# Linear attention and a Mish feed-forward in one kernel: the first loads in one queue and in other buffers, VectorE's work of a tile in other slots

## The chip, the cores and the metric

The kernel runs on one core of one Trainium2 chip. The metric is the device time of one execution in microseconds (us). TensorE (PE) multiplies, VectorE (DVE) and ScalarE (ACT) do the elementwise work, SyncE (SP) issues nearly all DMAs, GpSimd (POOL) only clears a few constants at the start. Each engine runs its instructions in the order in which the program lists them.

## The reference, cut to what matters

```python
kv  = einsum('bhsd,bhse->bhde', k, v)               # 8 batches, 8 heads, 576 tokens, head size 64
out = einsum('bhsd,bhde->bhse', q, kv)
rms = sqrt(mean(out * out, axis=-1) + 1e-6)
x   = (out / rms * g_norm) as [4608 tokens, 512]
h   = x @ w_in                                      # w_in 512 x 2048, float64 in memory
g   = h * tanh(log1p(exp(h)))                       # Mish
return g @ w_out                                    # w_out 2048 x 512, float64 in memory
```

## The kernel before, in words

Both large products are done by a scheme of Strassen's kind: seven block products instead of eight, on sums and differences of blocks. Each factor is split into a high part (`hi`, rounded to the matmul's format by a cast on ACT) and a rest (`lo`, a subtraction on DVE), and a product is three matmuls. So each operand costs one ACT cast and one DVE subtraction in `split` (lines 117 and 118).

**Part 1** makes h and Mish for 9 tiles of 512 tokens. A tile has 4 groups of 7 products: 28 **slots** a round, 9 rounds. A slot runs first the evictions that fall due (`evict`), then its product on PE (12 matmuls, line 472), then what the plan holds for that slot (`plan`, filled by `at(slot, f)`, in order of registration). This order, written out by hand, is the order on every engine; no planner moves anything. The evictions of a group are three copies and a Mish on ACT (lines 435, 440, 449, 114) and three additions on DVE (line 492, "put 11", "put 12", "put 22"). The product of A22 of a group is made two slots into the next group and accumulates onto the bank that "put 22" reads, so it waits for that addition.

In round j the kernel also prepares the x of tile j+1 ("attention", line 601), in two units of 4 heads: `load` of q (line 280, 4 or 8 DMAs), `transpose` on DVE (line 285), `halves` (a split), `project` on PE with the kept k-v products, `square` on ACT, `scaled` on DVE (line 324), `squares` (a split), `sums` on PE, `rstd` on ACT, `keep` (the factors to DRAM, line 361), `spread` (back to all partitions, line 368), `normalize` on DVE (line 376). Then `x_form` makes the seven operands of the tile (lines 390 to 409). Beside that, per round, the k-v products of one batch (`k_load`, `k_product`, `kv_keep`, line 232 on PE), and "out" chunks that turn a part of w_out into its seven block forms and store them in DRAM (line 198).

**Float64 weights** come as pairs of 32-bit words. `weight_forms` has the steps LOAD (4 DMAs of 256 KB, line 134), SCALE on ACT (line 139), JOIN (three DVE instructions on the raw words, lines 144 to 146), DIFF (154 to 156), BLOCKS and SUMS (splits). w_in has 8 chunks, of which group n of a tile uses 2n and 2n+1. Their raw words lie in one buffer of the pool `w64` (chunk 1 in a free `gf` buffer); the next LOAD can begin when the JOIN before it has read that buffer.

**Before slot 0** the kernel makes the x of tile 0 in one go (lines 530 to 575). The w_in and q loads go out on SP, those of the first k and v on ACT (`kv_load(nc.scalar, ...)`).

**Part 2** (from `part2`) makes the second product, g @ w_out, from what part 1 stored.

Of the kernel before, what the change touches and what calls it, by code (L numbers as in the profile page):

```python
# [26 lines left out]
def linear_attention_rms_mish_ffn(  # L27
# [239 lines left out]
    def unit_steps(j, u):  # L267
        st = {}

        def load():  # L270
# [77 lines left out]
        def rstd():  # L348
# [183 lines left out]
    kv0 = [kv_load(nc.scalar, 0, 4 * n, 4, [t for m in range(2) for t in (rooms[2 * n + m], rrooms[2 * n + m])]) for n in range(2)]
# [1 line left out]
    weights(1, LOAD)
# [66 lines left out]
    def attention(j):
# [6 lines left out]
        late = 2 if j == 1 else 0  # L608
        for u, n, *names in (
            (0, -19, "load"), (0, -1, "transpose"), (0, 0, "halves"), (1, 1, "load"), (0, 3, "project"),  # L610
            (0, 5, "square", "scaled"), (0, 6, "squares"), (1, 7, "transpose"), (0, 8, "sums"), (1, 9, "halves"),
            (1, 11, "project"), (1, 12, "square", "scaled"), (1, 13, "squares"), (1, 15, "sums"), (1, 16, "rstd"),
            (1, 17, "keep"), (0, 19, "spread0"), (0, 24, "normalize"), (1, 25, "normalize"),
        ):
            at(max(t + n + (late if n < 19 else 0), 0), lambda u=u, names=names: do(j, u, *names))
# [253 lines left out]
```

## Time and profile before

| | us |
|---|---|
| median of 3 runs (946.39 to 953.22) | 952.05 |
| the profiled execution, its own time | 948.55 |
| its span | 946.8 |
| PE busy in the span | 846.3 |
| DVE busy | 610.7 |
| ACT busy | 461.2 |
| mean granted TensorE clock, of full speed | 0.955 |

The span is what the profiler sees of the kernel; 1.75 us of the execution's time lie around it. Busy shares are averages over parts with different limits, so the prediction reads the kernel in stretches: the time up to the first product, then rounds, then part 2. PEclk in a row is the clock that TensorE was granted, 1.00 being 2.4 GHz and 0.50 being 1.2 GHz.

### The profile page before, as it was taken

The page shows a single profiled execution, that of the slowest core. Times are in us where ns is not written, and L with a number is a line of the kernel's source. Part 1 is how long each engine was busy: PE and PEld are TensorE (multiplying, and loading weights), DVE is VectorE, ACT ScalarE, POOL GpSimd, SP SyncE. Part 2 cuts the span into 40 slices and gives each one's busy share as a digit, 9 for nine tenths or more (in the row PEclk, how much of TensorE's full clock was granted, in tenths as well). Part 3 has the DMA queues.
Part 4 walks back from the last instruction along what each step waited for, and adds up shares of the span by engine and source line. Part 5 has one row for each costly group of instructions (what it writes and reads, how often), then busy time and mean ns, then how long its engine had stood idle before and what let it go on. Part 6 is the DMA issues. An engine that isn't in the chain of part 4 may idle for free. (4 is left out here: it accounts for less than half of the span.)

```text
span 946.8 us, 17029 instructions
## 1 busy us (share of the span) xinstructions
PE 846.3 (89%) x6940; PEld 809.7 (86%) x6940; DVE 610.7 (64%) x808; ACT 461.2 (49%) x698; POOL 4.3 (0%) x21
## 2 busy tenths in 40 slices
PE   2457598989799898979989979999999999999997
PEld 1246488989799898979989969999999999999997
DVE  2488567495674747567585435877667777667762
ACT  1445356656465665636666524444444344444341
POOL 1000000000000000000000000000000000000000
PEclk9769799999899899998999989999999999999999
DMA  9465666877869578668665799445443345443331
GB/s 251 118 177 153 198 197 194 238 240 233 237 211 282 173 231 275 198 196 226 205 182 173 248 402 388 146 135 166 129 129 113 112 149 163 122 125 111 113 111 45
DMA packets 157133, 177.40 MB, mean 187 GB/s; under 512 B 18752, under 2 KB 138560, under 8 KB 156032
## 3 DMA queue, kind: packets, MB, share of 16 engines
q1 hardware_dynamic: 153856, 173.97, 60.0%
q10 hardware_dynamic: 3200, 2.36, 1.0%
q8 instruction: 54, 0.88, 0.4%
q14 instruction: 23, 0.19, 0.1%
HBM read 114.30 MB, written 62.00 MB: 186 GB/s over the span
## 5 line engine op out<-in xcount | busy, mean ns | idle before, releaser
L697 PE MATMUL a<-wf,gf 128*128 128x256 f32 x1632 | 201.8, 283 | 0.5 <-DVE ur L728 0.5
L697 PEld LDWEIGHTS a<-wf,gf 128*128 128x128 f32 x1632 | 198.4, 192 | 0.7 <-DVE ur L728 0.7
L472 PE MATMUL a<-gf,wf 128*128 128x256 f32 x1296 | 180.3, 295 | 15.6 <-DVE gf L374 10.0
L118 DVE TENSOR_TENSOR gf<-g,gf 128x1024 fp32r<-128x1024 f32 (+1 forms) x123 | 132.9, 1087 | 87.9 <-ACT gf L117 87.9
L472 PEld LDWEIGHTS a<-gf,wf 128*128 128x128 f32 x1296 | 169.9, 201 | 19.5 <-issue 11.5
L472 PE MATMUL bc<-gf,wf 128*128 128x256 f32 x1296 | 174.7, 287 | 11.3 <-ACT ur L440 6.6
L472 PEld LDWEIGHTS bc<-gf,wf 128*128 128x128 f32 x1296 | 164.3, 194 | 16.8 <-ACT ur L440 6.8
L117 ACT CAST gf<-g 128x1024 fp32r<-128x1024 f32 (+1 forms) x123 | 114.4, 939 | 90.2 <-DVE g L677 65.1
L697 PE MATMUL bc<-wf,gf 128*128 128x256 f32 x1224 | 152.7, 283 | 0.1
L697 PEld LDWEIGHTS bc<-wf,gf 128*128 128x128 f32 x1224 | 149.4, 192 | 0.3 <-ACT gf L117 0.3
L472 PE MATMUL a<-a,wf 128*128 128x256 f32 x432 | 68.2, 314 | 38.5 <-DVE ur L492 38.5
L472 PEld LDWEIGHTS a<-a,wf 128*128 128x128 f32 x432 | 63.1, 217 | 44.0 <-DVE ur L492 41.0
L114 ACT ACTIVATE ur<-ur 128x1024 f32<-128x1024 f32 x36 | 38.1, 1058 | 52.7 <-DVE ur L492 52.7
L440 ACT COPY ur<-bc 128x512 f32<-128x512 f32 (+1 forms) x53 | 27.4, 517 | 39.7 <-PE bc L697 23.0
L492 DVE TENSOR_TENSOR ula<-bc,ula 128x512 f32<-128x512 f32 x36 | 24.8, 688 | 31.7 <-PE bc L472 13.8
L117 ACT CAST gf<-a 128x1024 fp32r<-128x1024 f32 x17 | 17.9, 1051 | 53.4 <-DVE a L674 53.4
L117 ACT CAST gf<-gf 128x512 fp32r<-128x512 f32 x45 | 27.0, 619 | 31.5 <-DVE gf L396 15.7
L118 DVE TENSOR_TENSOR gf<-gf 128x512 fp32r<-128x512 f32 x45 | 30.9, 688 | 17.1 <-ACT gf L117 17.1
L449 ACT COPY ur<-a 128x512 f32<-128x512 f32 (+1 forms) x53 | 27.5, 518 | 29.2 <-PE a L697 24.6
L118 DVE TENSOR_TENSOR fl<-fa,fh 128x1024 fp32r<-128x1024 f32 x28 | 34.2, 1221 | 11.3 <-ACT fh L117 11.3
L117 ACT CAST fh<-fa 128x1024 fp32r<-128x1024 f32 x28 | 29.2, 1043 | 10.5 <-DVE fa L285 9.7
L114 ACT ACTIVATE ula<-ula 128x512 f32<-128x512 f32 x36 | 22.7, 630 | 22.0 <-DVE ula L492 21.9
(130 smaller groups left out, 842.2 us busy)
## 6 DMA issues: line engine op xcount, KB each, us to landing
g<-gd SPq DMA_DIRECT2D x18, 2048.0 KB, 8.8
gd<-ur SPq DMA_DIRECT2D x36, 512.0 KB, 4.0
wod<-wst SPq DMA_DIRECT2D x16, 896.0 KB, 4.9
wf<-wod SPq DMA_DIRECT2D x8, 1792.0 KB, 14.4
gd<-ula SPq DMA_DIRECT2D x36, 256.0 KB, 3.9
gd<-ulb SPq DMA_DIRECT2D x36, 256.0 KB, 5.2
w<-in_moe_w_out_dram SPq DMA_DIRECT2D x32, 256.0 KB, 4.4
w<-in_moe_w_in_dram SPq DMA_DIRECT2D x28, 256.0 KB, 3.9
```

The source lines that it names most:

```text
L114: nc.scalar.activation(o, i, AF.Mish)
L117: nc.scalar.copy(hi, src)
L118: nc.vector.tensor_sub(lo, src, hi.bitcast(F32))
L440: then(t + 2, lambda: nc.scalar.copy(dst(st, "22"), st["c"]))
L449: then(t + 4, lambda: nc.scalar.copy(dst(st, "12"), st["a"]))
L472: nc.tensor.matmul(bank[:, jj], w[:, right, a, kc, :], xf[:, b, kc, :], start=first and jj == kc == s == 0, stop=(kc == 1 and s == 2), ski ...
L492: nc.vector.tensor_add(o, bank, o)
L697: nc.tensor.matmul(bank, gf[:, a, c, :], wo[c][:, right, b, :], start=first and c == s == 0, stop=(c == NF2 - 1 and s == 2), skip_group_ch ...
```

## The change

Before slot 0, all loads are issued on SP, in the order w_in chunk 0, k and v of heads 0 to 3, w_in chunk 1, q of unit 0, k and v of heads 4 to 7, q of unit 1, the norm's weights, w_in chunks 2 and 3. Chunks 1 to 3 and the second q go into buffers of the pool `wfp` (name `wf`) that hold no forms yet; the `gf` buffer `w1_room` is gone. DIFF, BLOCKS and SUMS of chunk 0 and SCALE and JOIN of chunk 1 stand ahead of the first transpose; SCALE, JOIN and DIFF of chunk 2 are done before slot 0.

In the rounds, steps stand in other slots: for tile 2 and later `transpose` of unit 0 in slot 20 of the round before (from 27), its `halves` in 25 (from 28), `normalize` in 23 and 24 (from 24 and 25), the operands in 24 to 31 (from 25 to 32), `kv_keep` in 14 (from 24), k-v products in 3, 6, 9, 12 (from 13, 16, 19, 22). The 16 out chunks begin in slots 6, 13, 20 of rounds 1 and 2 and in 9, 15 of rounds 3 to 7 (from every twelfth slot). Three names of buffers (`fh`, `fl`, `fa`) are swapped to fit.

```diff
-        def load():
-            t = qs[u] = att.tile([P, 2, T // R * D], F32, name="qs")
+        def load(t=None):
+            t = qs[u] = att.tile([P, 2, T // R * D], F32, name="qs") if t is None else t
...
-            t = att.tile([P, 2, T], F32, name="fh" if j < T32 else "fa")
+            t = att.tile([P, 2, T], F32, name="fh" if j < T32 else "fl")
...
-    w1_room = fp.tile([P, 4, 2 * P, 2], U32, name="gf")
...
+    early = {j: wfp.tile([P, 4, 2 * P, 2], U32, name="wf") for j in range(1, 4)}
+    early_q = wfp.tile([P, 2, T // R * D], F32, name="wf")
...
+    def k_first(n):
+        kv0.append(kv_load(nc.sync, 0, 4 * n, 4, [t for m in range(2) for t in (rooms[2 * n + m], rrooms[2 * n + m])]))
     weights(0, LOAD)
-    kv0 = [kv_load(nc.scalar, 0, 4 * n, 4, [...]) for n in range(2)]
+    k_first(0)
+    weights(1, LOAD)
     do(0, 0, "load")
-    weights(1, LOAD)
+    k_first(1)
+    units[0][1]["load"](early_q)
...
+    weights(2, LOAD)
+    weights(3, LOAD)
     kv_tiles()
...
     weights(0, SCALE, JOIN)
     kv_product(0, 0, 4, *kv0[0])
     kv_keep(0, slice(0, 2))
-    weights(0, DIFF)
-    do(0, 0, "transpose")
...
-    do(0, 0, "project")
-    weights(0, BLOCKS)
+    weights(0, DIFF, BLOCKS, SUMS)
+    weights(1, SCALE, JOIN)
+    do(0, 0, "transpose", "project")
+    weights(1, DIFF, BLOCKS)
     kv_product(0, 4, 4, *kv0[1])
     kv_keep(0, slice(2, 4))
     do(0, 0, "square", "sums")
-    weights(0, SUMS)
-    do(0, 1, "transpose", "project", "square")
+    weights(1, SUMS)
+    k_load(1, 0)
     k_load(1, 1)
+    weights(4, LOAD)
+    do(1, 0, "load")
+    do(0, 1, "transpose", "project")
     do(0, 0, "rstd")
...
+    weights(2, SCALE)
+    do(0, 1, "square", "sums")
     do(0, 0, "normalize")
+    weights(2, JOIN)
     x_form(A11)
+    do(0, 1, "rstd", "normalize")
     x_form(S1)
+    weights(2, DIFF)
+    for f, n in ((S2, 0), (A12, 1), (S4, 2), (S3, 3), (A22, 5)):
+        at(n, lambda f=f: x_form(f))
+    at(0, lambda: weights(2, BLOCKS, SUMS))
+    for j in range(3, NF2):
+        t = 3 * (j - 3) + 1
+        if 4 <= j < NF2 - 1:
             at(t + 1, lambda j=j: weights(j + 1, LOAD))
         for s, n in ((SCALE, 0), (JOIN, 0), (DIFF, 1), (BLOCKS, 1), (SUMS, 2)):
             at(t + n, lambda j=j, s=s: weights(j, s))
...
+        loads = (5, 6, 14, 16) if b == 2 else (20 - NS, 22 - NS, 5, 8) if b == 3 else (11 - NS, 15 - NS, 5, 8)
-            at(t + (13, 16, 19, 22)[p], lambda b=b, p=p: k_product(b, p))
-        at(t + 24, lambda b=b: kv_keep(b, slice(0, NKC)))
+            at(t + ((12, 14, 16, 18) if b == 2 else (3, 6, 9, 12))[p], lambda b=b, p=p: k_product(b, p))
+        at(t + (20 if b == 2 else 14), lambda b=b: kv_keep(b, slice(0, NKC)))
...
+            (0, 8 - NS if j > 2 else 9 - NS, "load"), (0, 20 - NS, "transpose"), (1, 22 - NS, "load"), (0, 25 - NS, "halves"),
+            (0, 0, "project"), (0, 3, "square", "scaled"), (0, 4, "squares"), (1, 5, "transpose"), (0, 6, "sums"),
+            (1, 8, "halves"), (1, 10, "project"), (1, 12, "square", "scaled"), (1, 13, "squares"), (1, 15, "sums"),
+        )
+        for u, n, *names in steps + ((1, 16, "rstd"), (1, 18, "keep"), (0, 19, "spread0"), (0, 23, "normalize"), (1, 24, "normalize")):
-        for f, n in zip(MADE, (25, 26, 27, 28, 29, 30, 32)):
+        for f, n in zip(MADE, (24, 26, 28, 29, 30, 30, 31)):
             at(t + n, lambda f=f: x_form(f))
...
-    for i in range(2 * NF2):
-        for s, n in zip(range(7), (-13, 0, 0, 1, 2, 3, 6)):
+    places = [NS * j + n for j in range(1, NT - 1) for n in ((6, 13, 20) if j < 3 else (9, 15))]
+    for i, t in enumerate(places):
+        for s, n in zip(range(7), (-12, 0, 0, 1, 2, 3, 5)):
```

## Rows read from the trace of the kernel before

**Rows 1.** Busy time by stretch: us, then PE, PEld, DVE, ACT, POOL, clock, DMA.
```profile
0.00:46.30 46.30, 16.52 (x96) 8.07 (x97) 16.54 (x22) 14.30 (x22) 4.33 (x21) 0.88 0.74 189
46.30:137.70 91.40, 64.46 (x509) 55.87 (x510) 64.56 (x89) 44.67 (x66) 0.00 (x0) 0.82 0.61 175
193.30:248.00 54.70, 51.60 (x451) 48.91 (x450) 35.28 (x54) 32.44 (x51) 0.00 (x0) 0.97 0.82 245
577.80:946.80 369.00, 363.58 (x3026) 363.00 (x3025) 256.73 (x275) 151.13 (x209) 0.00 (x0) 1.00 0.43 135
```
**Rows 2.** Timeline of PE, end of round 1: start, duration, instruction, idle time before.
```profile
199.84 2.93 PE L472 MATMUL a<-a,wf 128*128 128x256 f32 x12 [2.73 <-DVE ur L492]
202.57 1.72 PE L472 MATMUL a<-gf,wf 128*128 128x256 f32 x12
...
205.67 3.04 PE L472 MATMUL bc<-gf,wf 128*128 128x256 f32 x24
208.55 3.04 PE L472 MATMUL a<-gf,wf 128*128 128x256 f32 x24
```
**Rows 3.** Timeline of DVE, the same place.
```profile
197.97 1.24 DVE L285 STREAM_TRANSPOSE fa<-qs 128x1024 f32<-128x1024 f32 x1
199.13 0.65 DVE L492 TENSOR_TENSOR ur<-a,ur 128x512 f32<-128x512 f32 x1
```
**Rows 4.** Busy time, seven stretches of three products, the last and the sum.
```profile
474.52:484.24 9.72, 6.35 (x38) 5.95 (x38) 8.03 (x12) 6.44 (x11) 0.00 (x0) 0.82 0.71 183
sum 76.05, PE 47.24 PEld 44.29 DVE 63.55 ACT 47.32 POOL 0.00; mean PE 6.75 PEld 6.33 DVE 9.08 ACT 6.76 POOL 0.00
```
**Rows 5.** Busy time, the eighth such stretch.
```profile
526.14:531.33 5.19, 4.71 (x38) 4.43 (x38) 3.48 (x6) 4.35 (x8) 0.00 (x0) 1.00 0.28 113
```
**Rows 6.** Timeline of ACT before slot 0.
```profile
11.98 0.60 ACTq L212 DMA_DIRECT2D ulb<-in_v_dram  x1
12.77 1.13 ACT L139 ACTIVATE fl<-w 128x1024 f32<-128x1024 f32 x1 [10.74 <-DMA ula<-in_v_dram]
...
26.26 0.53 ACT L249 COPY kvf<-s 64x128 f32<-64x128 f32 x2 [8.16 <-PE s L232]
...
35.98 1.06 ACT L353 ACTIVATE fa<-fa 128x1024 f32<-128x1024 f32 x1
```
**Rows 7.** Timeline of PE before slot 0 and in round 0.
```profile
20.09 3.75 PE L308 MATMUL x<-fh,kvf 128*128 128x512 f32 x4 [5.50 <-DVE fh L285]
...
46.31 2.90 PE L472 MATMUL a<-gf,wf 128*128 128x256 f32 x12 [9.97 <-DVE gf L374]
...
68.28 1.12 PE L232 MATMUL s<-vm,km 128*64 128x64 f32 x16 [8.62 <-DMA vm<-in_v_dram]
...
113.29 2.93 PE L472 MATMUL a<-a,wf 128*128 128x256 f32 x12 [10.59 <-DVE ur L492]
```
**Rows 8.** What the spread's transfers (line 368) took: min, median, max.
```profile
DMA to landing us min/median/max: 3.8/5.2/6.5
```
**Rows 9.** DMA of the first 24 us.
```profile
DMA packets 5857, 6.01 MB, mean 250 GB/s; under 512 B 1370, under 2 KB 5466, under 8 KB 5857
```
**Rows 10.** Timeline of all engines, one chunk of w_in to the next.
```profile
69.01 1.23 DVE L146 SCALAR_TENSOR_TENSOR fl<-w,fl 128x1024 uint32<-128x1024 uint32 x1
...
70.30 2.44 SPq L134 DMA_DIRECT2D w<-in_moe_w_in_dram  x4
...
76.67 1.16 ACT L139 ACTIVATE fl<-w 128x1024 f32<-128x1024 f32 x1
...
79.85 1.22 DVE L146 SCALAR_TENSOR_TENSOR fl<-w,fl 128x1024 uint32<-128x1024 uint32 x1
```
**Rows 11.** Timeline of DVE before slot 0.
```profile
41.20 1.40 DVE L374 SCALAR_TENSOR_TENSOR gf<-x,gcol,fa 128x512 f32<-128x512 f32 x2
```
**Rows 12.** Busy time of DVE on a chunk of w_in: us, DVE, clock, DMA.
```profile
13.90:20.90 7.00, 6.75 (x9) 1.00 1.08 265
```
**Rows 13.** Busy time in round 8 around PE's longest wait there, seven products.
```profile
547.16:566.55 19.39, 12.60 (x85) 12.19 (x83) 4.78 (x13) 4.97 (x12) 0.00 (x0) 0.82 1.01 406
```

More of the change, by code (lines that the diff above doesn't have):

```diff
@@ L289, in parts @@
             hi = att.tile([P, 2, T], F32R, name="fh")
-            lo = att.tile([P, 2, T], F32R, name="fl")
+            lo = att.tile([P, 2, T], F32R, name="fa")
             split(hi, lo, t)
@@ L315, in square @@
         def square():
-            st["s"] = att.tile([P, 2, T], F32, name="fh" if j == 0 and u else "fa")
+            st["s"] = att.tile([P, 2, T], F32, name="fl" if j >= T32 else "fh" if j == 0 and u else "fa")
             if "x2" in st:
@@ L354, in rstd @@
                 return
-            r = st["r"] = att.tile([H, T], F32, name="fa")
+            r = st["r"] = att.tile([H, T], F32, name="fa" if j < T32 else "fl")
             nc.scalar.preload_act_table_set("natural_log_exp_and_others")
@@ L510, in linear_attention_rms_mish_ffn @@
     rrooms = [up.tile([SL, 4, D], F32, name=n) for n in ("ula", "ula", "ulb", "ulb")]
+    early = {j: wfp.tile([P, 4, 2 * P, 2], U32, name="wf") for j in range(1, 4)}
+    early_q = wfp.tile([P, 2, T // R * D], F32, name="wf")
     def w64_room():
         return pools["w64"].tile([P, 4, 2 * P, 2], U32, name="w64")
-    conv = {j: weight_in(j, (lambda: w1_room) if j == 1 else w64_room) for j in range(NF2)}
+    conv = {j: weight_in(j, (lambda j=j: early[j]) if 0 < j < 4 else w64_room) for j in range(NF2)}
     LOAD, SCALE, JOIN, DIFF, BLOCKS, SUMS, STORE = range(7)
@@ L530, in linear_attention_rms_mish_ffn @@
     nc.scalar.preload_act_table_set("natural_log_exp_and_others")
+    kv0 = []
+    def k_first(n):
+        kv0.append(kv_load(nc.sync, 0, 4 * n, 4, [t for m in range(2) for t in (rooms[2 * n + m], rrooms[2 * n + m])]))
     weights(0, LOAD)
[L532 removed]
+    k_first(0)
+    weights(1, LOAD)
     do(0, 0, "load")
[L534 removed]
+    k_first(1)
+    units[0][1]["load"](early_q)
+    for r in (slice(0, D), slice(D, P)):
+        nc.sync.dma_start(gcol[r, :], g_norm.rearrange("(p o) -> p o", o=1))
+    weights(2, LOAD)
+    weights(3, LOAD)
     kv_tiles()
@@ L607, in attention @@
         t = NS * (j - 1)
[L608 to L615, printed above, removed]
-        for f, n in zip(MADE, (25, 26, 27, 28, 29, 30, 32)):
+        steps = (
+            (0, 1, "transpose"), (1, 3, "load"), (0, 5, "project"), (0, 7, "square", "scaled"), (1, 7, "transpose"),
+            (0, 9, "sums"), (1, 11, "project"), (1, 13, "square", "scaled"), (1, 15, "sums"),
+        ) if j == 1 else (
+            (0, 8 - NS if j > 2 else 9 - NS, "load"), (0, 20 - NS, "transpose"), (1, 22 - NS, "load"), (0, 25 - NS, "halves"),
[3 more added lines that the diff above has]
+        for u, n, *names in steps + ((1, 16, "rstd"), (1, 18, "keep"), (0, 19, "spread0"), (0, 23, "normalize"), (1, 24, "normalize")):
+            at(t + n, lambda u=u, names=names: do(j, u, *names))
+        for f, n in zip(MADE, (24, 26, 28, 29, 30, 30, 31)):
             at(t + n, lambda f=f: x_form(f))
@@ L631, in run @@
                 conv["out", i][s]()
-            at(max(NS - 2, NS + 6 + 12 * i + n), run)
+            at(max(NS - 2, t + n), run)
     wo = [None] * NF2
```

24 lines of the change are left out of this document (2 added, 22 removed).

## The prediction

> **What bounds the kernel now.** I read busy time by stretch first [rows 1]. Part 2, 369 us of the span, has PE busy for 363.6 at clock 1.00: the change touches nothing there, so its time stays. Two stretches are not bound by PE. The first 46.3 us run to the first product; round 0 then takes 91.4 us with PE busy for 64.5 and DVE for 64.6. A later round takes 54.7 us, PE busy for 51.6.
>
> Next the timeline of PE at a round's end [rows 2]. PE waits 2.73 us for DVE's line 492, and the 12 matmuls behind it take 2.93 us; at full pace 24 take 208.55 − 205.67 = 2.88, so a product takes 1.44. The reader should see two losses: the wait, and a product at half clock after it. DVE shows the cause [rows 3]: the addition that PE waits for ("put 22") stands behind the next tile's transpose, and behind that the operands of slots 25 to 32. The seven ends of rounds 0 to 6, measured over the same three products (slots 29 to 31 and their like), take 76.05 us [rows 4] where 7 × 3 × 1.44 = 30.2 would do: 45.8 us are lost. The eighth end takes 5.19, loses 0.9 and keeps clock 1.00 [rows 5]. That one has the same operands to make, but no further tile's transpose and halves, no `kv_keep` and no out chunk. It is the nearest thing the trace has to the changed order.
>
> Last the start [rows 6, 7]: SCALE of chunk 0 begins at 12.77, once ACT has issued its last DMA (11.98 to 12.58); the first product waits for `normalize` until 46.31. In round 0 PE waits 8.62 us for a v load and 10.59 for put 22, the latter held up by a late chunk of w_in.
>
> **The change, part by part.**
>
> *Ends of rounds.* Per tile, transpose and `halves` of unit 0 (1.24 us on DVE each, the halves as the transpose) and `kv_keep` leave slots 24 to 28, the normalisations and operands start one slot earlier, and S1 is made before put 22 falls due. From slot 28 on DVE has put 22 first, then one or two operands a slot. So each of the seven ends should look like the eighth: 7 × 0.9 = 6.1 us remain. The ends of rounds 1 and 2 get a third out chunk in slots 20 to 23. With three evictions, the transpose, two normalisations, a `halves` and two operands, some 14.5 us of DVE work stand in eight slots of 1.44, 11.5 us. Put 22 is then 3 us late and has two products (2.9 us) of slack. I charge 1.5 us to each of the two. Gain 45.8 − 6.1 − 3 = **36.7 us**; ends of the unknown: 45.8 (nothing left) and 23 (half stays).
>
> What the moved steps run into: k-v products and out chunks go to slots 3 to 18, where PE in such a round is busy without a gap and DVE has room (35.3 of 54.7 us). `keep` moves to slot 18, `spread` stays at 19, `normalize` comes one slot earlier. A spread lands 3.8 to 6.5 us after its issue [rows 8], and slots 19 to 23 are 5.8 us, so DVE may wait up to 1 us. Behind it queue the operand A11, the halves, put 11; A11 is not used before slot 28, which hides it. If that cover is gone, it is 1 us a round. The transpose in slot 20 newly waits for the `keep` transfer to have read `fl`; put 22 of slot 21 stands behind it, and PE asks for that in slot 23.
>
> *The start.* All first loads move from two queues to SP: 16 DMAs of k and v and w_in chunks 2 and 3 more, 34 with those that were there. Chunk 0 (1024 KB) no longer shares with k, and ACT issues nothing. At 250 GB/s [rows 9] and a start at 2 us, chunk 0 lands near 6, the first k and v (1152 KB) near 11, chunk 1 near 15, q near 19, the second k and v near 24, the second q near 28, chunk 2 (7.54 MB in all) near 32. Then along the new order: SCALE of chunk 0 at 6, JOIN (1.1 + 3.2 as in [rows 10]) to 10.4, the rest of chunk 0, behind two `kv_keep` copies on ACT, to 17.4, JOIN of chunk 1 to 20.6, transpose to 21.8, `project` 3.75 to 25.6, the second k-v product 2.4 (from 23.84 to the copy at 26.26 [rows 6, 7]) to 28. That copy is then 1.8 us later than before. Before, the first product came 20.0 us after that copy. In that time `normalize` of unit 0 was ready at 37.0 (35.98 + 1.06) but ran at 41.2 [rows 6, 11], behind JOIN of chunk 1: 4.2 us. DIFF of that chunk (1.5 of its 6.75) stood ahead of the second one, and ACT put `square` of unit 1 (1.1, as SCALE) ahead of `rstd` of unit 0. These go: 7 us. JOIN of chunk 2 comes in, while DVE waits for the second `rstd` anyway. First product near 28 + 13 = 41: gain **5.3 us**. Ends: 10 (k and v land early enough that PE never waits for them) and −2 (at 189 GB/s, the mean of the whole first stretch, chunk 2 lands at 42, is needed at 34.5, and SCALE holds up ACT until then).
>
> For these loads row and rule can be weighed. The row shows ACT held by its own DMA issues until 12.58 [rows 6]. The Trainium skill ("DMA: Bandwidth & Descriptors", "Issuing engines are not separate DMA queues") says that DMAs of all issuing engines run on the same 16 engines and that a second issuer saves only issue time, usually small. By it, leaving ACT's queue costs no bandwidth and freeing ACT brings next to nothing: the start's gain would be 0 and the sum 5 us less. That the issue was not small here is what the row has against it.
>
> *Round 0.* A chunk of w_in costs DVE about 6.75 us [rows 12] (there JOIN, DIFF and BLOCKS with a transpose, which takes as long as SUMS). With one raw buffer, one JOIN follows the other by the loop load, SCALE, JOIN: 81.07 − 70.24 = 10.83 us [rows 10]. Before, six chunks go through that loop. After, chunk 2 is half done, 3 and 4 are loaded, three loops remain. From the first product F, DVE has S1 and the rest of chunk 2, chunk 3, JOIN of chunk 4 (together two chunks, 13.5), a transpose, and S2, A12, S4, S3 at 0.7 an instruction, with some 2.5 us of waits for ACT's casts: JOIN of chunk 4 ends near F + 23.6. Three loops later, F + 56.1, JOIN of chunk 7 in slot 13 ends; `scaled` and put 22 follow, 2.0 us (as the two of [rows 3]); A22 of slot 16 waits for that, runs at half clock (2.9), and eleven products (15.8) and two k-v products (1.9) later slot 28 begins, at F + 79. Gain 91.4 − 79 = **12.3 us**. The 8.62 us wait for v goes or shrinks, without a term of its own: DVE sets the pace there. Ends: 20 (each loop as fast as DVE's 6.75) and 4 (SP holds a load back twice by some 4 us, behind the q loads it is queued with).
>
> *Round 8 and part 2*: nothing; the 9 us lost in round 8 [rows 13] come from the loads of part 2, which stay.
>
> Sum: 36.7 + 5.3 + 12.3 = 54.3. The profiled execution took 948.55 (span 946.8), so 894.3; the median of the runs lies 3.5 higher: **898 us**.
>
> **The rivals.**
>
> *The waits move* (chance 0.17). DVE's work in slots 14 to 23, and a `normalize` waiting for its spread, hold put 11 and put 22 elsewhere. [...] Against: the eighth end. Half of the 45.8 stays and the start gives half: 952 − 23 − 9 = 920, between 915 and 942.
>
> *Transfers bound the rounds, no change* (0.06). A round of 54.7 us has the DMA engines busy for 0.82 of it, 44.9 us [rows 1]; a third out chunk in rounds 1 and 2 adds about 3.5. That is 48 under a round of about 50 us, so close that queueing may take back what DVE gives: the rounds stay, the start gives 0 to 8, 944 to 952.
>
> *SP's one queue holds the stores back* (slower, 0.07). In the rounds SP takes q loads in slots 8 and 22, k loads in 5, 8, 11 and 15 and the out chunks, each waiting its turn for a buffer, with the stores of Mish behind it. A `ur` buffer that isn't stored stops ACT's copy and then PE. Round 8 shows the price: 19.39 us for seven products that need 10.1 [rows 13], so 9.3. Over seven rounds that is 65, against a gain of 54: 963. It turns the sign above 54 / 7 = 7.8 us a round. Against: there the DMA engines were full (1.01), in rounds they are at 0.82.
>
> That the edit doesn't do what it says has little room: evictions stand ahead of the plan in each slot, so put 22 does precede slot 28's operand.
>
> **How the numbers follow.** The forecast's own case (884 to 915) gets 0.66, a better one below 0.04. The range takes in the bounds and the larger part of the first rival: 882 to 932, which leaves out 0.2. This kernel's measurement can tell about 1% (9.5 us). Faster 0.87, within 1% 0.06, slower 0.07.
>
> **What would show it.** Stretches of three products at rounds' ends of 5 to 7 us at clock 1.00, no PE wait on line 492 above 1 us in slot 30; first product at 39 to 43; round 0 near 79 us; rounds 1 to 5 near 50. A first product at 46 or later would mean that the loads are bound by bandwidth; rounds of 54 with PE waiting for ACT's copies, that SP is late. The prediction is wrong if the ends of rounds lose as much elsewhere.

## The result, and the profile after

The changed kernel takes 902.04 us (median of 4 runs, 899.57 to 903.71). The kernel before, beside it, took 952.19 (946.39 to 953.22): a ratio of 0.948, with a 95% interval of 0.944 to 0.953. The profiled execution took 899.57, its span 897.8, at a mean clock of 0.98.

Busy time by stretch of the kernel after, to set beside [rows 1]: up to the first product, rounds 0 to 3, round 8, part 2.

```profile
0.00:40.64 40.64, 14.11 (x96) 7.18 (x96) 21.84 (x28) 16.73 (x24) 4.32 (x21) 1.00 0.99 254
40.64:117.74 77.10, 62.91 (x508) 52.09 (x509) 63.02 (x87) 43.38 (x66) 0.00 (x0) 0.89 0.71 194
117.74:172.35 54.61, 51.76 (x450) 49.29 (x449) 38.31 (x61) 33.76 (x55) 0.00 (x0) 0.97 0.87 252
172.35:229.12 56.77, 52.77 (x450) 49.98 (x449) 39.98 (x65) 33.94 (x56) 0.00 (x0) 0.94 0.87 255
229.12:279.10 49.98, 49.56 (x451) 47.25 (x450) 35.45 (x54) 32.16 (x52) 0.00 (x0) 1.00 0.85 254
475.10:528.84 53.74, 44.45 (x350) 43.64 (x349) 19.45 (x37) 20.97 (x38) 0.00 (x0) 0.94 0.91 334
528.84:897.80 368.96, 363.52 (x3026) 362.93 (x3024) 256.60 (x274) 151.18 (x209) 0.00 (x0) 1.00 0.43 135
```

The start is 5.7 us shorter (46.31 to 40.64), round 0 by 14.2 (91.3 to 77.1). Rounds 1 to 7, measured the same way in both traces, together lose 29.5: 55.55, 54.65, 57.48, 57.03, 55.31, 55.27, 51.62 became 54.61, 56.77, 49.98, 49.90, 50.80, 47.70, 47.60. Round 8 is 0.4 longer, part 2 the same. That is 49.0 of 948.55 − 899.57 = 48.98. Note what does not fit the pattern: round 1 has gained only 0.9 us and round 2 has lost 2.1, while round 3 stands at a PE busy for 49.56 of 49.98.

The same seven ends of rounds as in [rows 4], in the kernel after: the last stretch and the sum.

```profile
430.35:434.67 4.32, 4.32 (x38) 4.31 (x37) 2.30 (x4) 3.06 (x6) 0.00 (x0) 1.00 1.09 389
sum 30.49, PE 30.49 PEld 30.11 DVE 15.26 ACT 22.40 POOL 0.00; mean PE 4.36 PEld 4.30 DVE 2.18 ACT 3.20 POOL 0.00
```

76.05 us have become 30.49, and PE is busy for all of them: three products at full pace are 4.32. Nothing is left of the loss.

PE in the kernel after (start, duration, instruction, idle time before it and what ended that): the start as in [rows 7], the v load, the products of slots 13 and 14 of round 1 and its longest wait, the longest wait of round 2, the same two rows of round 3, round 8.

```profile
23.13 3.44 PE L308 MATMUL x<-fh,kvf 128*128 128x512 f32 x4 [8.21 <-DVE fh L285]
...
40.64 1.69 PE L471 MATMUL a<-gf,wf 128*128 128x256 f32 x12 [2.65 <-DVE gf L374]
...
50.80 1.12 PE L232 MATMUL s<-vm,km 128*64 128x64 f32 x16 [4.95 <-DMA vm<-in_v_dram]
...
145.51 3.14 PE L471 MATMUL a<-gf,wf 128*128 128x256 f32 x24
...
159.26 4.62 PE L471 MATMUL a<-gf,wf 128*128 128x256 f32 x24 [2.48 <-ACT ur L448]
...
215.06 5.49 PE L471 MATMUL a<-gf,wf 128*128 128x256 f32 x24 [3.56 <-ACT ur L448]
...
255.70 3.13 PE L471 MATMUL a<-gf,wf 128*128 128x256 f32 x24
...
267.37 3.13 PE L471 MATMUL a<-gf,wf 128*128 128x256 f32 x24 [0.42 <-ACT ur L448]
...
510.48 2.93 PE L471 MATMUL bc<-gf,wf 128*128 128x256 f32 x12 [7.44 <-ACT ur L439]
```

At the ends of rounds PE no longer waits for line 491 (492 before). Elsewhere five waits for that addition are left, 6.2 us in all, the longest of 3.7 us in slot 9 of round 0. What is new is slot 20 of rounds 1 and 2: there PE waits for ACT's copy of line 448, and the two products behind it take 4.62 and 5.49 us, where those of round 3 take 3.13.

ACT in the kernel after: SCALE of chunk 0 and the first copy of the second `kv_keep`, as in [rows 6]; then the work ahead of the copy of line 448 in round 1; one row of it in round 2; the same work in round 3.

```profile
7.70 1.12 ACT L139 ACTIVATE fl<-w 128x1024 f32<-128x1024 f32 x1 [5.67 <-DMA w<-in_moe_w_in_dram]
...
28.37 0.53 ACT L249 COPY kvf<-s 64x128 f32<-64x128 f32 x2 [5.58 <-PE s L232]
...
149.66 0.37 ACT L117 CAST kv<-s 64x256 fp32r<-64x256 f32 x1 [3.23 <-DVE kv L118]
150.05 1.06 ACT L114 ACTIVATE ur<-ur 128x1024 f32<-128x1024 f32 x1
...
152.56 0.61 ACT L117 CAST wst<-wx 128x128 fp32r<-128x128 f32 x2 [0.84 <-DMA wod<-wst]
...
158.62 0.58 ACT L448 COPY ur<-a 128x512 f32<-128x512 f32 x1
...
208.37 0.61 ACT L117 CAST wst<-wx 128x128 fp32r<-128x128 f32 x2 [1.91 <-DMA wod<-wst]
...
258.67 0.37 ACT L117 CAST kv<-s 64x256 fp32r<-64x256 f32 x1 [2.48 <-DVE kv L118]
259.06 1.06 ACT L114 ACTIVATE ur<-ur 128x1024 f32<-128x1024 f32 x1
...
266.73 0.59 ACT L448 COPY ur<-a 128x512 f32<-128x512 f32 x1
```

DVE in the kernel after: JOIN of chunks 4 and 7 of w_in in round 0, then the place in round 1 for which ACT waited 3.23 us.

```profile
62.46 1.23 DVE L146 SCALAR_TENSOR_TENSOR fl<-w,fl 128x1024 uint32<-128x1024 uint32 x1
...
94.91 1.23 DVE L146 SCALAR_TENSOR_TENSOR fl<-w,fl 128x1024 uint32<-128x1024 uint32 x1
...
146.83 0.42 DVE L144 TENSOR_SCALAR wx<-wx 128x512 uint32<-128x512 uint32 x1
...
148.01 0.69 DVE L146 SCALAR_TENSOR_TENSOR wx<-w,wx 128x512 uint32<-128x512 uint32 x1
148.62 0.68 DVE L491 TENSOR_TENSOR ur<-a,ur 128x512 f32<-128x512 f32 x1
149.22 0.41 DVE L118 TENSOR_TENSOR kv<-s,kv 64x256 fp32r<-64x256 f32 x1
```

Read the last three fences together, and set rounds 1 and 2, in which an out chunk begins in slot 13, beside round 3, in which none does. In round 1 the JOIN of that chunk runs on DVE ahead of put 22 and of a k-v subtraction, and ACT's Mish (line 114) follows these. All times are in us.

| | round 1 | round 2 | round 3 |
|---|---|---|---|
| from the start of slot 13's product to Mish | 4.54 | 4.54 | 3.36 |
| from Mish to the copy of line 448 | 8.57 | 9.64 | 7.67 |
| in that, ACT's wait for the store of the out chunk before | 0.84 | 1.91 | none |
| PE's wait in slot 20 | 2.48 | 3.56 | 0.42 |

Of what PE waits more than in round 3 (2.1 and 3.1 us), 1.2 us are the late Mish behind JOIN, and 0.9 and 2.0 us are added on ACT, whose cast for the chunk waits until the chunk before has been stored from the same buffer (`wst`). The 3.23 us for which ACT waits for DVE are not the delay: in round 3 it waits 2.48 in the same place. A delay of DVE arrives on PE ten microseconds later under ACT's name.

### The profile page after: what moved, and what is told of

Its sections match the earlier page's. It is cut to its first block, busy times and chain, and to the rows that moved or that the text cites. A ratio compares the mean times of both kernels' runs of the same rounds, so it can differ in the third digit from the quotient of the medians.

```text
span 897.8 us, 17035 instructions
## 1 busy us (share of the span) xinstructions
PE 831.1 (93%) x6940; PEld 796.0 (89%) x6940; DVE 613.7 (68%) x808; ACT 459.2 (51%) x698; POOL 4.3 (0%) x21
## 5 line engine op out<-in xcount | busy, mean ns | idle before, releaser
L471 PE MATMUL a<-gf,wf 128*128 128x256 f32 x1296 | 177.3, 291 | 12.2 <-ACT ur L448 9.4
L471 PEld LDWEIGHTS a<-gf,wf 128*128 128x128 f32 x1296 | 166.5, 197 | 20.0 <-ACT ur L448 11.5
L471 PE MATMUL bc<-gf,wf 128*128 128x256 f32 x1296 | 170.8, 286 | 8.4 <-ACT ur L439 7.4
L471 PEld LDWEIGHTS bc<-gf,wf 128*128 128x128 f32 x1296 | 162.4, 192 | 10.1 <-ACT ur L439 7.6
L471 PE MATMUL a<-a,wf 128*128 128x256 f32 x432 | 59.3, 288 | 6.2 <-DVE ur L491 6.2
L471 PEld LDWEIGHTS a<-a,wf 128*128 128x128 f32 x432 | 55.9, 194 | 10.0 <-DVE ur L491 4.9
L114 ACT ACTIVATE ur<-ur 128x1024 f32<-128x1024 f32 x36 | 38.1, 1059 | 40.4 <-DVE ur L491 40.2
L118 DVE TENSOR_TENSOR fa<-fl,fh 128x1024 fp32r<-128x1024 f32 x28 | 34.2, 1222 | 22.1 <-ACT fh L117 21.2
L491 DVE TENSOR_TENSOR ula<-bc,ula 128x512 f32<-128x512 f32 x36 | 24.7, 687 | 23.5 <-PE bc L471 18.2
L117 ACT CAST fh<-fl 128x1024 fp32r<-128x1024 f32 x28 | 29.4, 1048 | 0.0
```

Of the source, the lines that this page charges most:

```text
L114: nc.scalar.activation(o, i, AF.Mish)
L117: nc.scalar.copy(hi, src)
L118: nc.vector.tensor_sub(lo, src, hi.bitcast(F32))
L471: nc.tensor.matmul(bank[:, jj], w[:, right, a, kc, :], xf[:, b, kc, :], start=first and jj == kc == s == 0, stop=(kc == 1 and s == 2), ski ...
L491: nc.vector.tensor_add(o, bank, o)
```

## The experiments

Each is the changed kernel with the edit shown, except e2. Times are medians. The last five columns come from the profiled execution, in us: the start of the first product, then the time from there to the start of the A22 product of slot 30 (two slots into round 1), from that to the one of slot 86 ("rounds 1, 2"), to the one of slot 226 ("rounds 3 to 7") and to the last, of slot 252.

| | us (range) | ratio to before [95%] | first product | to slot 30 | rounds 1, 2 | rounds 3 to 7 | to slot 252 |
|---|---|---|---|---|---|---|---|
| before | 952.19 (946.39–953.22) | 1 | 46.3 | 98.3 | 112.6 | 270.8 | 48.3 |
| after | 902.04 (899.57–903.71) | .948 [.944, .953] | 40.6 | 81.7 | 111.1 | 244.5 | 49.3 |
| e1 old rounds | 930.66 (928.48–931.72) | .981 [.977, .984] | 42.2 | 82.5 | 113.2 | 271.4 | 48.8 |
| e2 old start | 918.72 (916.91–922.42) | .969 [.965, .973] | 44.7 | 97.8 | 108.1 | 244.8 | 49.8 |
| e3 two queues | 903.17 (899.28–903.81) | .951 [.947, .955] | 43.8 | 84.5 | 108.6 | 244.5 | 49.2 |
| e4 late chunks | 902.03 (901.62–903.36) | .951 [.948, .954] | 42.1 | 82.5 | 100.6 | 254.0 | 50.3 |
| e5 attention back | 912.88 (911.68–914.99) | .962 [.960, .965] | 40.6 | 81.0 | 113.5 | 254.6 | 49.7 |
| e6 operands back | 902.19 (899.34–903.75) | .951 [.947, .955] | 41.5 | 82.4 | 108.5 | 246.4 | 48.3 |
| e7 k-v back | 915.03 (911.64–918.21) | .964 [.961, .968] | 42.1 | 83.7 | 109.1 | 254.7 | 49.5 |
| e8 middle chunk | 898.81 (898.21–902.06) | .948 [.945, .951] | 41.6 | 83.1 | 106.0 | 245.3 | 49.6 |
| e9 out back | 914.76 (911.38–915.42) | .965 [.962, .967] | 41.9 | 83.1 | 105.3 | 259.3 | 49.4 |
| e10 attention, k-v back | 916.69 (911.53–919.24) | .966 [.962, .970] | 42.8 | 82.6 | 110.1 | 261.5 | 50.1 |
| e11 middle and load | 894.65 (891.82–896.40) | .944 [.941, .947] | 40.2 | 82.4 | 105.2 | 245.2 | 44.3 |
| e12 only out new | 919.43 (917.58–920.47) | .969 [.966, .971] | 44.9 | 80.3 | 110.7 | 262.9 | 48.3 |

**e1, the new start with the old rounds.** From tile 2 on, every moved step stands where it stood before.

```diff
-            (0, 8 - NS if j > 2 else 9 - NS, "load"), (0, 20 - NS, "transpose"), ..., (0, 25 - NS, "halves"),
+            (0, -20 if j > 2 else -19, "load"), (0, -1, "transpose"), (0, 0, "halves"), ...
-        for f, n in zip(MADE, (24, 26, 28, 29, 30, 30, 31)):
+        for f, n in zip(MADE, (25, 26, 27, 28, 29, 30, 32) if j > 1 else (24, 26, 28, 29, 30, 30, 31)):
...
+            at(t + ((12, 14, 16, 18) if b == 2 else (13, 16, 19, 22))[p], lambda b=b, p=p: k_product(b, p))
+        at(t + (20 if b == 2 else 24), lambda b=b: kv_keep(b, slice(0, NKC)))
...
+        t = NS + 6 + 12 * i
```

> The changed start and round 0, but from tile 2 on every step (attention, normalize, operands, k-v products, kv_keep, out chunks) in its old slot. Theory A (two gains that add up: start and round 0 give 20 us, the slots of rounds 1 to 7 give 29): about 931 us; first product still at 40 to 41 us, round 0 still 77, the ends of rounds 1 to 6 lose 5 to 8 us each again with PE waiting for line 492. Rival B (the rounds gain mostly because the earlier start lets loads run ahead): below 915 us.

930.66 us: 28.6 above the changed kernel. PE of e1, one end of a round:

```profile
180.13 2.05 PE L471 MATMUL a<-a,wf 128*128 128x256 f32 x12 [2.74 <-DVE ur L491]
```

The wait of [rows 2] (2.73) is back at the ends of six rounds: 2.74, 5.5, 2.73, 2.73, 5.5, 2.72.

**e2, the old start with the new rounds.** The kernel before, with the new slots from tile 2 on.

```diff
-            at(t + (13, 16, 19, 22)[p], lambda b=b, p=p: k_product(b, p))
-        at(t + 24, lambda b=b: kv_keep(b, slice(0, NKC)))
...
+            at(t + ((13, 16, 19, 22) if b == 2 else (3, 6, 9, 12))[p], lambda b=b, p=p: k_product(b, p))
+        at(t + (24 if b == 2 else 14), lambda b=b: kv_keep(b, slice(0, NKC)))
...
+        ) if j == 1 else (
+            (0, 8 - NS if j > 2 else 9 - NS, "load"), (0, 20 - NS, "transpose"), (1, 22 - NS, "load"), (0, 25 - NS, "halves"),
...
+    places = [NS * j + n for j in range(1, NT - 1) for n in ((6, 13, 20) if j < 3 else (9, 15))]
```

> The old start and round 0 (two queues, w1_room, old places of tile 1), with the new slots from tile 2 on and the new places of the out chunks. Theory A: 952 - 25 to 29 = 923 to 927 us, rounds 3 to 7 at 47 to 51 us, first product at 46, round 0 at 91. Rival B (the rounds need the early loads): rounds 3 to 7 stay above 53 us, total above 940.

918.72, 4 us below the range of theory A. The start with round 0 is worth 1.95% alone (e1), the rounds 3.13% alone (e2); together 5.1%, and both were 5.2%. The two halves of the change add up.

**e3, k and v on ACT's queue again**, in the new order and buffers.

```diff
-        kv0.append(kv_load(nc.sync, 0, 4 * n, 4, ...))
+        kv0.append(kv_load(nc.scalar, 0, 4 * n, 4, ...))
```

> The changed kernel with the first k and v loads issued by ACT again. Theory A (ACT's issue of its own DMAs holds up SCALE of chunk 0, and two queues share the transfers so that chunk 0 lands later): SCALE at 12 to 13 us instead of 7.7, first product 3 us later at 43 to 44, total 904 to 906. Rival C (the issuing engine doesn't matter, the order of the transfers is what counts and the chain through k, v and project hides SCALE): first product within 0.7 us of 40.6, total within 1 us of the changed kernel.

903.17, which cannot be told from the changed kernel. ACT of e3:

```profile
11.22 0.61 ACTq L212 DMA_DIRECT2D ulb<-in_v_dram  x1
12.01 1.14 ACT L139 ACTIVATE fl<-w 128x1024 f32<-128x1024 f32 x1 [9.99 <-DMA ula<-in_v_dram]
```

Issuing the DMAs holds ACT as in [rows 6], and SCALE of chunk 0 is 4.3 us late (12.01 after 7.70). The first product comes 3.1 us later in this profile, as theory A had it, yet the totals do not show it: the runs of the two kernels cover the same range. The last section takes this delay apart.

**e4, the third out chunk in rounds 6 and 7** instead of 1 and 2. The slots change with it: 6, 13 and 20 where a round has three chunks, 9 and 15 where it has two. Rounds 6 and 7 have no `kv_keep`.

```diff
-    places = [NS * j + n for j in range(1, NT - 1) for n in ((6, 13, 20) if j < 3 else (9, 15))]
+    places = [NS * j + n for j in range(1, NT - 1) for n in ((9, 15) if j < 6 else (6, 13, 20))]
```

> The changed kernel with the third out chunk of rounds 1 and 2 moved to rounds 6 and 7 (slots 9 and 15 in rounds 1 to 5, 6, 13 and 20 in rounds 6 and 7). Theory D (the waits of 2.5 and 3.6 us at slot 20 of rounds 1 and 2 come from the out chunk of slot 13 meeting kv_keep and rstd on ACT): rounds 1 and 2 fall from 54.6 and 56.8 to 50 to 51 us, rounds 6 and 7, which have no kv_keep, rise by 0 to 3 us: total 891 to 897. Rival E (rounds 1 and 2 are slow for what precedes them, the transfers of the start still queued): they stay above 53 us, total at 902 or more.

902.03, no change in the total (theory D expected 891 to 897), but the waits have moved with the chunk. PE of e4, rounds 6 and 7:

```profile
410.48 3.14 PE L471 MATMUL a<-gf,wf 128*128 128x256 f32 x24 [1.76 <-ACT ur L448]
...
463.20 4.63 PE L471 MATMUL a<-gf,wf 128*128 128x256 f32 x24 [2.03 <-ACT ur L448]
```

Rounds 1 and 2 take 100.6 us (111.1), rounds 3 to 7 254.0 (244.5). So three chunks in these slots cost about 5 us more than two, in either pair of rounds, and `kv_keep` is not needed for it. In rounds 6 and 7 put 22 of slot 14 begins 1.2 and 0.9 us later than in the changed kernel, and PE's wait in slot 20 is 1.2 and 1.1 us longer.

**e5, attention's steps back alone.**

```diff
-            (0, 8 - NS if j > 2 else 9 - NS, "load"), (0, 20 - NS, "transpose"), ..., (0, 25 - NS, "halves"),
+            (0, -20 if j > 2 else -19, "load"), (0, -1, "transpose"), (0, 0, "halves"), ...
```

> The changed kernel with the attention steps of tile 2 and later in their old slots (transpose in 27, halves in 28, project in 3 and so on); normalize, operands, k-v products and out chunks stay new. Theory F (it is the operands' own time, 25 to 32, that put DVE behind at a round's end): ends of rounds lose 0 to 1.5 us, total 903 to 912. Rival G (it is the transpose and the halves ahead of put 22, as the prediction had it): ends of rounds lose 3 to 5 us again with PE waiting for line 491, total 922 or more.

912.88: 10.8 worse, about 2 us a round, between the two theories and not by the old wait. PE of e5, an end of a round:

```profile
290.46 1.69 PE L471 MATMUL a<-gf,wf 128*128 128x256 f32 x12 [1.51 <-ACT ula L434]
```

PE waits for ACT's copy, one slot later than in [rows 2]. ACT of e5 just before:

```profile
287.41 0.62 ACT L117 CAST gf<-gf 128x512 fp32r<-128x512 f32 x1 [3.15 <-DVE gf L395]
...
289.84 0.56 ACT L434 COPY ula<-a 128x512 f32<-128x512 f32 x1
```

ACT has waited 3.15 us for an operand (line 395), 1.1 more than at such ends in the changed kernel (2.02). DVE makes it behind the transpose of slot 27, here at 284.98 to 286.2, and put 22. The same late step is paid for through the other engine.

**e6, the operands of S and A back alone**, with the normalisations.

```diff
+        for u, n, *names in steps + (..., (0, 24 if j > 1 else 23, "normalize"), (1, 25 if j > 1 else 24, "normalize")):
...
-        for f, n in zip(MADE, (24, 26, 28, 29, 30, 30, 31)):
+        for f, n in zip(MADE, (25, 26, 27, 28, 29, 30, 32) if j > 1 else (24, 26, 28, 29, 30, 30, 31)):
```

> The changed kernel with normalize in 24 and 25 and the operands in 25 to 32 for tile 2 and later, everything else new. Theory F: DVE has normalize, halves, S1 and S2 (10 us with three evictions) ahead of put 22 in slots 24 to 27, so PE waits 2 to 4 us for line 491 at each round's end and loses the clock after it: total 916 to 930. Rival G: ends lose 0 to 1.5 us, total 903 to 912.

902.19, no change, less than either theory allowed for. Waits for line 491 do come back at ends of rounds: 1.6 us at two ends, 0.4 to 0.6 at three, none at two. PE of e6:

```profile
232.45 1.69 PE L471 MATMUL a<-a,wf 128*128 128x256 f32 x12 [1.59 <-DVE ur L491]
```

The 12 matmuls behind this wait take 1.69 us; in [rows 2], behind a wait of 2.73, they took 2.93. That the operands' slots alone carry the gain is wrong: put back alone, they bring some waits for line 491 and cost nothing that the total shows.

**e7, the k-v products and `kv_keep` back alone.**

```diff
-        loads = (5, 6, 14, 16) if b == 2 else (20 - NS, 22 - NS, 5, 8) if b == 3 else (11 - NS, 15 - NS, 5, 8)
+        loads = (5, 6, 14, 16) if b == 2 else (20 - NS, 23 - NS, 14, 17)
-            at(t + ((12, 14, 16, 18) if b == 2 else (3, 6, 9, 12))[p], lambda b=b, p=p: k_product(b, p))
-        at(t + (20 if b == 2 else 14), lambda b=b: kv_keep(b, slice(0, NKC)))
+            at(t + ((12, 14, 16, 18) if b == 2 else (13, 16, 19, 22))[p], lambda b=b, p=p: k_product(b, p))
+        at(t + (20 if b == 2 else 24), lambda b=b: kv_keep(b, slice(0, NKC)))
```

> The changed kernel with the k-v products of batch 3 and later in slots 13, 16, 19 and 22, their loads in the old slots and kv_keep in 24. Theories F and G both: kv_keep adds 1.3 us on DVE ahead of normalize, two k-v products (1.8 us) give DVE time before slot 24: ends lose 0 to 2 us, total 902 to 912. If the waits at slot 20 of rounds 1 and 2 need kv_keep in slot 14 they go, and the total falls to 896 to 900; if the JOIN of the out chunk in slot 13 alone makes them, they stay at 2 us or more.

915.03: 13.0 worse, above the 902 to 912 that both theories expected. The waits of slot 20 in rounds 1 and 2 are gone. By the expectation that would be a sign that they need `kv_keep` in slot 14, but put 22 is later here than in the changed kernel (2.5 us after slot 13's product ends, 1.4 there); the three k-v products now in slots 13 to 19, some 1 us each on PE, leave ACT that time. Rounds 3 to 7 lose 10.2. Waits of `normalize` (line 376) for the spread of unit 0, in all and how many, first of the kernel after, then of e7:

```profile
  DMA fh<-rd: 3.0, 4
```
```profile
  DMA fh<-rd: 11.1, 5
```

For both units they are 7.7 us in the kernel after and 14.7 in e7. The old k loads of slots 14 and 17 (5 and 8 in the changed kernel) stand on SP ahead of `keep` and `spread`. That these waits make the whole 10.2 is not shown. DVE of e7, one of these five:

```profile
276.87 1.23 DVE L376 TENSOR_TENSOR gf<-gf,fh 128x1024 f32<-128x1024 f32 x1 [3.34 <-DMA fh<-rd]
```

**e8, the middle chunk of rounds 1 and 2 three slots earlier**, and the first with it, so that no JOIN stands ahead of put 22 and the k-v casts of slot 14.

```diff
-    places = [... for n in ((6, 13, 20) if j < 3 else (9, 15))]
+    places = [... for n in ((3, 10, 20) if j < 3 else (9, 15))]
```

> The changed kernel with the out chunks of rounds 1 and 2 in slots 3, 10 and 20 instead of 6, 13 and 20. Theory H (JOIN of slot 13 stands ahead of put 22 on DVE, Mish waits for that on ACT, and rstd and the copy of slot 18 behind it come late): PE's waits at slot 20 of rounds 1 and 2 go below 1 us, these rounds take 50 to 52 us instead of 54.6 and 56.8, total 893 to 898. Rival I (a third chunk is 4 to 6 us too much for ACT, DVE or the transfers of a round, wherever it stands): rounds 1 and 2 stay at 54 or more, total 900 to 904.

The waits of slot 20 are gone, as expected, and rounds 1 and 2 take 106.0 us (111.1; theory H expected 100 to 104). New is a wait of 1.1 us in slot 9 of each. PE of e8, round 1:

```profile
139.94 1.70 PE L471 MATMUL a<-a,wf 128*128 128x256 f32 x12 [1.10 <-DVE ur L491]
```

That the waits of slot 20 hang on the chunk of slot 13 is thereby shown. The links go by the traces: put 22 begins 0.65 and 0.46 us earlier behind slot 13's product than in the changed kernel, and from Mish to the copy of line 448 it takes 6.62 us (8.57 and 9.64), as the chunk's casts and the wait for a store no longer stand in that stretch of ACT. The total (898.81, ratio .948) cannot be told from the changed kernel's; in this profile the start and round 0 took 2.4 us longer.

**e9, the out chunks back alone**, one every 12 slots.

```diff
-    for i, t in enumerate(places):
-        for s, n in zip(range(7), (-12, 0, 0, 1, 2, 3, 5)):
+    for i in range(2 * NF2):
+        t = NS + 6 + 12 * i
+        for s, n in zip(range(7), (-13, 0, 0, 1, 2, 3, 6)):
```

> The changed kernel with the out chunks every twelfth slot again (34, 46, 58, 70, 82, ...), everything else new. Theory J (no single step makes the ends of rounds lose; DVE ahead of put 22 has some slack, and each step put back takes a part of it): JOIN of slot 82 and 166 (slot 26 of rounds 2 and 5) stands ahead of put 22, those two ends lose 1 to 3 us, the waits at slot 20 of rounds 1 and 2 go (no chunk in 13): total 897 to 903. Rival K (the out chunks at rounds' ends were the main cause): every end with a chunk in slots 26 to 30 loses 4 us or more, total 915 or more.

914.76, 12.7 worse; the theory that expected 897 to 903 missed, and the rival's 915 was nearly met, though not by the 4 us that it named for each end with a chunk. PE of e9:

```profile
233.55 1.69 PE L471 MATMUL a<-gf,wf 128*128 128x256 f32 x12 [1.49 <-ACT ula L434]
...
324.94 1.69 PE L471 MATMUL a<-a,wf 128*128 128x256 f32 x12 [1.89 <-DVE ur L491]
```

A chunk every 12 slots falls on a different place of each round, and each of rounds 3 to 7 loses 2 to 4 us against the changed kernel, some of it at its end.

**e10, attention and k-v back together.**

```diff
+            at(t + ((12, 14, 16, 18) if b == 2 else (13, 16, 19, 22))[p], lambda b=b, p=p: k_product(b, p))
+        at(t + (20 if b == 2 else 24), lambda b=b: kv_keep(b, slice(0, NKC)))
...
+            (0, -20 if j > 2 else -19, "load"), (0, -1, "transpose"), (0, 0, "halves"), ...
```

> The changed kernel with the attention steps and the k-v products with kv_keep in their old slots, operands and out chunks new. Each alone cost 10.8 and 13.0 us. Theory J: together they cost at least their sum, as the slack is gone: 924 to 931, nearly all of the 28.6 us that all steps together gave. If the parts cost separately by kind (attention: the wait for the ACT copy after project; k-v: time on PE), they add to 926 without any wait for line 491 at a round's end; if put 22 is what is late, PE waits 1 us or more for line 491 in slot 30 of rounds 2 to 6.

916.69: 14.7 worse. The 924 to 931 that their costs alone (23.8 together) give missed. PE of e10, an end of a round:

```profile
289.45 1.70 PE L471 MATMUL a<-a,wf 128*128 128x256 f32 x12 [0.74 <-DVE ur L491]
...
293.08 2.45 PE L471 MATMUL a<-gf,wf 128*128 128x256 f32 x12 [1.92 <-ACT ula L434]
```

**e12, only the out chunks new**: e10 with `normalize` and the operands back too.

```diff
+        for u, n, *names in steps + (..., (0, 24 if j > 1 else 23, "normalize"), (1, 25 if j > 1 else 24, "normalize")):
...
+        for f, n in zip(MADE, (25, 26, 27, 28, 29, 30, 32) if j > 1 else (24, 26, 28, 29, 30, 30, 31)):
```

> The changed kernel with attention, normalize, operands, k-v products and kv_keep all in their old slots from tile 2 on; only the out chunks keep their new places. It differs from the run with attention and k-v back (916.7 us) by the operands alone, and from the one with everything back (930.7) by the out chunks alone. Theory J (steps share one slack, so a step that is free alone costs once others are back): operands cost 3 us or more now, 920 to 928, and PE waits for line 491 in slot 30 by 2 us or more. Rival N (operands never matter; the out chunks make the rest): 915 to 918, and the out chunks alone account for 13 to 15 us.

919.43, between the totals of the two theories. PE of e12, the same end:

```profile
290.54 2.27 PE L471 MATMUL a<-a,wf 128*128 128x256 f32 x12 [2.74 <-DVE ur L491]
```

With the operands in their old slots the wait is again the 2.74 us for line 491, as theory J had it, and the product behind it is slower (2.27). That costs 2.7 us more than e10, too little to be told apart (the ranges overlap). From e12 to e1 only the out chunks differ: 11.2 us, with ranges apart.

**e11, e8 with the g load of part 2 thirteen slots later in round 8.**

```diff
-    at(t8 + 8, lambda: g_load(1))
+    at(t8 + 21, lambda: g_load(1))
```

> The out chunks in slots 3, 10 and 20 of rounds 1 and 2 as in the run with the middle chunk (898.8 us), and the second load of part 2's operand (2 MB, g_load(1)) in slot 21 of round 8 instead of 8. Theory L (the wait of 7.4 us in round 8 is a Mish store queued behind the loads of part 2, which move 400 GB/s there): 2 MB less ahead of it is 5 us, the wait falls to 2 to 3 us and round 8 from 49.6 to 44 or 46; total 893 to 896. Rival M (the transfers of round 8 must all be there before part 2 begins, so that the wait only moves to its end): round 8 and the start of part 2 together stay within 1 us, total 898 to 900.

894.65, the fastest kernel of all: its slowest run (896.40) is below the fastest of the changed kernel (899.57), though the intervals of the ratios overlap, and below the fastest of e8 (898.21), from which only the load differs. PE of e11, round 8 and part 2:

```profile
500.53 2.93 PE L471 MATMUL bc<-gf,wf 128*128 128x256 f32 x12 [2.77 <-ACT ur L439]
...
538.56 2.78 PE L790 MATMUL q<-wf,gf 128*128 128x256 f32 x21 [1.85 <-DMA wf<-wod]
```

The wait of 7.44 is down to 2.77, as theory L expected, and a wait of 1.85 us comes up in part 2.

## Why the prediction was right

The forecast was 898, the median is 902.04; of the forecast gain of 54.3 us 49.0 came between the profiled executions. By its steps:

- **Ends of rounds.** The cause was named rightly: put 22 behind the transpose, halves and operands (e1 and e12 bring the wait back, the new order takes it away). It takes them together: with the attention's steps back but not the operands, the wait for line 491 at an end is at most 0.76 us (e5, e10), with the operands back alone at most 1.6 (e6), with both 2.7 (e12). The eighth end was a bound, not the value: I left 6.1 us in the seven ends, and 30.49 − 30.2 = 0.3 remain, 5.8 better.
- **The third out chunk: the term of the sum that was mis-sized, and in the wrong place.** "I charge 1.5 us to each of the two", 3 us, at put 22 behind the chunk of slots 20 to 23. There nothing was lost: the ends of rounds 1 and 2 take 4.46 and 4.32 us. But rounds 1 and 2 are 4.6 and 6.8 us longer than round 3, 11.4 in all, and what I can follow of it is lost at the middle chunk, in slot 13. That one was among the steps moved to slots 3 to 18, which I put at nothing because DVE "has room" by its mean over a round; the JOIN stands ahead of put 22 all the same. I had looked only for the instruction that PE awaits from DVE. The delay passes to ACT, where the wait for a store adds to it, and comes to PE as a wait for ACT's copy. PE's waits in slot 20 are 5.2 us longer than in round 3, and the slower products behind them (4.62 and 5.49, in round 3 3.13) are another 3.9; the other 2.3 I have not followed. e4 measures the term by moving it (10.5 less in rounds 1 and 2, 9.5 more later), e8 takes 5.1 of it away.
- **Small waits elsewhere.** Rounds 1 to 7 lost 29.5 where the ends gave 45.6. Beside the 11.4, that leaves some 4.6, for which I had no term; PE's waits of 0.4 to 0.9 us in rounds 3 to 7 add to 4.3. The first rival ("the waits move"), which named DVE's work in slots 14 to 23 ahead of put 22, so came true in part, at 16 us, not at half of 45.8.
- **The moved steps.** The cover named for `normalize` held: it waits for spreads ten times, 7.7 us in all, and no PE wait at an end of a round follows. What I did not price is what the k loads would cost in slots 14 and 17 once the rest is new: in e7 these waits are 14.7 us.
- **The start.** SCALE of chunk 0 at 7.70 (6), the copy at 28.37 (28), the first product at 40.64 (41). 5.7 us, forecast 5.3. That is partly luck: at like clocks the start gains 4.1 to 4.2 (last section). With round 0 it is 19.9, forecast 17.6; e1, which has only this part, is 1.95% faster than before, 18.6 us (15 to 22 by its interval).
- **Round 0.** From the first product to the end of JOIN of chunk 4 23.05 us (23.6), of chunk 7 55.5 (56.1), the three loops 10.5, 11.3 and 10.6 (10.83). The round took 77.1, forecast 79; the wait for v is 4.95 (8.62 before).
- **Round 8 and part 2**: nothing, and nothing it was (0.4). That the loads of part 2 make the long wait of round 8 is borne out by e11, which moves one of them.

With these: 54.3 + 5.8 (ends) − 8.4 (third chunk) − 4.6 (small waits) + 0.4 (start) + 1.9 (round 0) − 0.4 (round 8) = 49.0.

The two other rivals fell. Transfers do not bound the rounds: round 3 takes 50 us with the DMA engines at 0.85 and PE busy throughout. SP holding stores back would stop ACT's copies, and PE after them, in every round; in rounds 3 to 7 no such wait reaches 1 us. Its sign, rounds of 54 us with PE waiting for ACT's copies, did come in rounds 1 and 2 (54.6 and 56.8, where I had named 50). There it is DVE's JOIN, and besides the store of an out chunk, that makes the copies late. Whether that store lands late for SP's order or for the transfer itself is not shown.

On the first loads, the row of e3 says that ACT is held by its own issues until 11.83 and SCALE is 4.3 us late. The Trainium skill ("DMA: Bandwidth & Descriptors", "Issuing engines are not separate DMA queues") says that another issuer brings no bandwidth and saves only issue time, usually small. The totals agree (903.17 and 902.04). The start that gains nothing, which I drew from the rule, did not come, and the rule does not say it: it speaks of the issuer alone, while 7 us of my sum for the start were steps put in another order on DVE and ACT, which e3 keeps. How much of the start's gain is the issuer's, the totals cannot tell.

**What stays open.** Alone, undoing attention, operands, k-v and out chunks costs 10.8, 0.2, 13.0 and 12.7, together 36.7; undoing all four costs 28.6. The runs show that they overlap (attention and k-v 14.7 instead of 23.8) and that the engine PE waits for changes from one to the other. A count of what each saves by itself does not exist. Why the third chunk's 5 us a round remain in part in e8, and why its shorter rounds do not show clearly in the total, isn't settled.

## What to carry to other kernels

When an addition is late on the engine that feeds TensorE, look for what stands ahead of it in program order and move that into slots with slack; a neighbouring stretch without those steps gives a good bound. Then follow each delay on to the engine that waits for the delayed one: here 1.2 us on DVE, and one to two more on ACT, reached PE ten microseconds later under ACT's name, with slower products behind it. A wait that looks long is not yet a delay: compare it with the same place in a stretch that runs well. Don't add up what parts of a reordering are worth alone: price each with the others in place.

## What the runs showed of the hardware

The first product came between 40.2 and 44.9 us in the eleven kernels whose code before slot 0 is the same (all but before, e2 and e3). The clock differs. Busy time (us, PE, PEld, DVE, ACT, POOL, clock, DMA): of the kernel after and of e4 from 27 to 34 us, and of e12 from 34 to 40.

```profile
27.00:34.00 7.00, 3.94 (x38) 2.08 (x33) 2.50 (x3) 5.06 (x8) 0.00 (x0) 1.00 1.00 287
```
```profile
27.00:34.00 7.00, 5.24 (x44) 2.63 (x42) 2.38 (x2) 3.16 (x5) 0.00 (x0) 0.77 0.91 276
```
```profile
34.00:40.00 6.00, 5.28 (x6) 2.02 (x7) 4.71 (x6) 3.78 (x6) 0.00 (x0) 0.50 0.95 280
```

The four `sums` matmuls took 1.95 us at the higher of the two levels and 3.55 in e4, and the waits ahead of them were the same. The three kernels with a clock of 1.00 from 27 to 40 us (after, e5, e11) have their first product at 40.2 to 40.6, e4 at 42.1, e12 at 44.9. The old start varies too. The kernel before and e2, which has the same start, from 27 to 34 us:

```profile
27.00:34.00 7.00, 5.42 (x8) 1.71 (x8) 2.38 (x2) 2.06 (x3) 0.00 (x0) 0.76 0.99 283
```
```profile
27.00:34.00 7.00, 5.01 (x11) 1.84 (x11) 2.38 (x2) 2.51 (x5) 0.00 (x0) 1.00 0.94 278
```

Their first products came at 46.31 and 44.72. So at a clock of 1.00 in this stretch the new start gains 4.1 us (44.72 to 40.64), at 0.76 and 0.77 it gains 4.2 (46.31 to 42.07); the 5.7 of the two main profiles compares a slower stretch with a faster one. A single profile of a start is good to some 4 to 5 us, and the forecast's 41 was met with some luck.

In e3 not all is clock. Until 27 us it is 1.00 there as in the others, but `project` begins at 24.80 where it begins at 22.4 to 23.5 in the eleven: 1.3 to 2.4 us are lost by then, behind the late SCALE. The rest of the late first product (43.77) falls in stretches with a clock of 0.95 and 0.77 (27 to 34 and 34 to 40 us).

Nor does each wait cost a slow product besides: behind 2.65 us of waiting the first product of the kernel after took 1.69 us, behind 2.73 in [rows 2] one took 2.93.
